# One PSUM tile handed out by the schedule, a shared buffer for the squares, stored priorities and a shorter first inverse in a Nyström attention + MLP kernel

## The chip, the cores and the metric

The kernel runs on one core of a Trainium2 chip. The metric is the device time of one execution in microseconds (us). A core has TensorE (PE; its weight loads are listed apart as PEld), VectorE (DVE), ScalarE (ACT), GpSimd (POOL) and SyncE (SP). [...]

## The reference

Queries, keys and values have 8 batches, 8 heads, 576 tokens and 64 values per head. Attention goes through 32 landmarks per head, each the mean of 18 tokens, and an inverse of a 32x32 matrix by six Newton steps. The result feeds an MLP with squared ReLU of width 2048.

```python
q_lm = q.reshape(B, H, 32, 18, D).mean(axis=3); k_lm = k.reshape(B, H, 32, 18, D).mean(axis=3)
A  = sm(q, k_lm)       # sm(a, b) = softmax(a @ b.T / 8)
Bm = sm(q_lm, k_lm)
C  = sm(q_lm, k)
Z  = Bm.T / (norm1(Bm) * norminf(Bm) + 1e-6)
for _ in range(6):
    Z = 2 * Z - Z @ Bm @ Z
x = (A @ Z @ C @ v)    # heads side by side: 4608 rows of 512
h = x @ w_in           # 512 x 2048
out = np.maximum(h, 0) ** 2 @ w_out   # 2048 x 512
```

## The kernel before

**Batches.** Eight batches go through three stages: `attention(b)`, `mlp_in(b)`, `mlp_out(b)`. The kernel never forms the attention's output. `attention` makes `AT`, the normalized left softmax in bf16 (tokens along the free dimension), and `WT`, the product of the inverse with C·v, and then multiplies `WT` with `w_in` into `G` (heads' landmarks by 2048). `mlp_in` multiplies `G` with `AT` into `h` (128 rows of the hidden width at a time, f = 0 to 15, each 576 tokens in two pieces of 288), ACT takes the ReLU into `r` (L1055) and DVE squares it into `gT` (L1058). `mlp_out` multiplies `gT` with `w_out` into tiles `o` of 128 tokens by 512 (16 matmuls each), which ACT or DVE copies out and SP stores. Names such as L1112 are lines of this kernel. Batches are paired: 576 is four tiles of 128 tokens and 64 left over, and the left-overs of an even and an odd batch make one `mid` tile, from two buffers `gTs[0]` and `gTs[1]`, as 32 matmuls on 64-column halves of the PE array (L1099, L1101).

**The planner.** Nobody writes the order of work by hand. Each operation is added to a `Plan` with its engines and costs, what it reads and writes, a priority, a PE tile mode ("full", "64x32", ...), and the PSUM rings that it takes a buffer from. `Plan.schedule` simulates a list schedule: of the ready operations it takes the one that can start first, then critical ones (the whole of `attention(0)` up to G is critical), then by priority. Priorities rise with the batch, so later batches' attention is spread between earlier batches' MLP. A change of PE's tile mode costs 98 ns in the plan (`SWITCH`). `search(700)` tries 700 random shifts of the priorities and keeps the best plan. The instructions are then issued in the plan's order on each engine, and each engine runs its own in order.

**PSUM.** Three rings of two buffers: `h` (two banks each; `mlp_in`, left scores `sa`, their sums `ss`, and G), `n` (one bank; the small matmuls of the inverse) and `o` (one bank; output tiles, and in batch 0 the key scores `sc`).

**The first attention.** Batch 0 has nothing to hide behind. k's first half comes by SP in float32 (`kst`) and is cast by both ACT and DVE; k's second half and q's two halves come through POOL's queue. While the load is under way, PE multiplies zeros (46 matmuls in `warm`). POOL makes the masks (`constants`), DVE the other constants (`constants2`, L438 to L456), which the copies of the segment sums (`part`) wait for under the key "cst". `fold_mm` (L603) adds the two halves of the sums, `b_mm` (L626) makes the landmark scores, ACT and DVE make the softmax Y0. The inverse goes through a chain of `blocks` (L657: eight 32x32 matmuls in mode "32x32") and DVE steps (`scaled`, `double`): Y1 to Y5 and Z. `cv_mm` (L872) multiplies the exponentials `EC` with v in three steps, into unused columns of the banks of the left scores (`sa`, 1), so it waits until ACT has read those (`Ea`). Four copies (`cvb`) and the reciprocal `rcv` follow, then Z4T, `u` 4 = Z4T·cvb, `u` 5 = 2·u4 + Y4·u4 (one block and one `double`, L915), `wt_mm2` (L970) = u5·Y5, a copy to `WT`, G's first 512 columns (L982), their copies (L325, L323), and the first `in_mm` at L1044. A block may be preceded by `fill` matmuls on zeros, up to its `busy` number (2 for qq 1 to 4, 1 for u 4 and 5, else 0), where the plan sees PE idle for more than 225 + 187 ns.

**Loads.** POOL issues in order: k, q, v of batch 0, w_in 0 and 1, k and q of batch 1, w_in 2 and 3, w_out 0 and 1, v of batch 1, w_out 2 and 3. Output tiles use w_out piece f // 4 for row block f, and those of batch 0 are computed in two halves of f, added by DVE.

**Later batches.** Per batch, four operations on PE are not in mode "full": the left scores `a_mm` (L824), `cv_mm` (L890), and two `g_two` (L982), each of which takes two `h` buffers and computes 2 x 512 columns of G; its second eight matmuls use a form (`again`) without a weight load of their own. The rest of the inverse runs on PE in mode "full".

Of the kernel before, what the change touches and what calls it, by code (L numbers as in the profile page):

```python
# [9 lines left out]
P = 128  # L10
# [7 lines left out]
B = 8  # L18
H = 8
# [14 lines left out]
LAG = 1.0  # L34

# [6 lines left out]
class Plan:  # L42
# [8 lines left out]
    RINGS = {"h": 2, "n": 2, "o": 2}  # L51
# [3 lines left out]
    SWITCH = 98.0  # L55
    DMA_NS_PER_BYTE = 1.0 / 410.0
    SLACK = 150.0
    FILL, HOLD = (225.0, 187.0), 1500.0
# [67 lines left out]
    def schedule(self, shift=None):  # L126
# [12 lines left out]
        ring = {r: [] for r in self.RINGS}  # L139
# [16 lines left out]
        while left:  # L156
# [11 lines left out]
            for op in ready:  # L168
                t0 = ready_at[op]
                ok = True  # L170
                if op.acq:
                    for rn in set(r for r, _ in op.acq):
                        want = sum(r == rn for r, _ in op.acq)
                        n = len(ring[rn]) + want - self.RINGS[rn]
                        for x in range(max(n - want, 0), max(n, 0)):
                            if ring[rn][x] not in freed:
                                ok = False
                                break
                            t0 = max(t0, freed[ring[rn][x]])
                    if not ok:  # L180
                        continue
                for e, dur in op.eng.items():
# [14 lines left out]
                    key = (t, not op.crit, prio[op], op.idx, dur, fill)  # L197
                    if best is None or key < best[0]:
                        best = (key, op, e, dur)
            if best is None:  # L200
                return 1e9, log
            (t, _, _, _, dur, op.fill), op, e, _ = best
# [12 lines left out]
            for rn, k in op.acq:  # L215
                ring[rn].append(k)
# [17 lines left out]
            for k in op.keys:  # L234
# [3 lines left out]
                if not pending[k]:  # L238
                    freed[k] = freed_at
        return max(op.end for op in self.ops), log  # L240

    def search(self, rounds):

        rng = random.Random(1)
        n = len(self.ops)
        best = [0.0] * n
        end, log = self.schedule(best)
        for _ in range(rounds):
            shift = list(best)
            if rng.random() < 0.5:  # L250
                a, w, d = rng.randrange(n), rng.choice((1, 3, 10, 40)), rng.gauss(0.0, 0.15)
                for i in range(a, min(a + w, n)):
                    shift[i] += d
            else:
                for _ in range(rng.choice((1, 4, 16))):
                    shift[rng.randrange(n)] += rng.gauss(0.0, 0.15)
            e, x = self.schedule(shift)
            if e <= end:
# [940 lines left out]
```

The softmax here doesn't subtract the row's maximum and nothing guards it: scores larger than these inputs give would overflow.

## Time and profile before

| | |
|---|---|
| median of 7 runs | 255.54 us (255.22 to 257.16) |
| the profiled execution | 255.47 us, span 253.8 us, mean PE clock 0.98 |
| PE busy | 243.9 us, 2701 matmuls |
| DVE, ACT, POOL busy | 174.8, 164.4, 28.3 us |
| `o` matmuls L1112 | x528, 132.0 us |
| `mid` matmuls L1099 and L1101 | x64 each |
| `in_mm` L1044 and L315 | x256 each, 67.2 us each |
| ReLU on ACT L1055, square on DVE L1058 | x128, 651 ns and 452 ns each |
| DMA | 35.59 MB; the 16 engines 90% busy or more in slices 2 to 12 of 40 |

The span runs from the first to the last instruction; the time also holds what lies around it. In the page, "PEclk" is the PE clock that was granted, in tenths, in 40 slices of 6.3 us. The stage table gives, for each stretch, the length, each engine's busy time with its number of instructions, the granted clock, the DMA share and GB/s. The timeline gives start and length in us, engine, line, operation, output<-inputs, tile shape (rows*columns of the array), operand shape, count, and in brackets the engine's idle time before it and what ended it. Matmuls overlap: the distance between starts tells PE's pace, not the length of one.

### The profile page before, as it was taken

What the parts mean: (1) busy time and instruction counts of PE and PEld (TensorE: products, weight loads), DVE (VectorE), ACT (ScalarE), POOL (GpSimd) and SP (SyncE); (2) the same over time, 40 slices, a digit from 0 to 9 for tenths busy, and PEclk for the clock granted to TensorE, in tenths of its full rate; (3) what the DMA queues carried; (4) which work ended last, traced back from release to release, by engine and by line L of the source; (5) the groups of instructions that cost most, each with busy time, mean ns of one, the idle gap of its engine ahead of it and who ended that gap; (6) DMA issues with size and microseconds to landing.
All of it is one profiled execution on the core that took longest, in us unless ns stands there. A gap on an engine that the chain in (4) does not pass through costs nothing.

```text
span 253.8 us, 6615 instructions
## 1 busy us (share of the span) xinstructions
PE 243.9 (96%) x2701; PEld 144.9 (57%) x2701; DVE 174.8 (69%) x487; ACT 164.4 (65%) x282; POOL 28.3 (11%) x51
## 2 busy tenths in 40 slices
PE   8777999999999999999999999999999999999994
PEld 7653775456644655565645565467466544565453
DVE  1865778759966898799897799979966762253000
ACT  3586798567942887677865985769688744474211
POOL 7822200003003000300300040010000000000000
PEclk9975999999999999999999999999999999999999
DMA  7999999999998998699599969996110131301233
GB/s 141 186 206 204 207 205 208 172 169 184 179 157 188 198 200 165 112 204 230 96 187 216 146 89 220 220 163 124 44 41 3 44 83 41 85 0 41 85 83 83
DMA packets 57054, 35.59 MB, mean 140 GB/s; under 512 B 29760, under 2 KB 52544, under 8 KB 57024
## 3 DMA queue, kind: packets, MB, share of 16 engines
q0 software_dynamic: 22672, 18.06, 47.5%
q1 hardware_dynamic: 34352, 17.11, 32.2%
q8 instruction: 21, 0.34, 0.5%
q14 instruction: 9, 0.07, 0.1%
HBM read 36.70 MB, written 9.44 MB: 182 GB/s over the span
## 4 chain that ended last, share of the span: by engine, by line
PE 89%; DVE 5%; ACT 2%; DMA 2%; issue 1%; DVEq 0%
PE o L1112 43%; PE h L315 14%; PE h L1044 12%; PE o L1099 6%; PE n L842 2%; PE h L982 2%; DMA kst<-in_k_dram 2%; PE n L890 1%; PE n L794 1%; PE o L315 1%; PE h L824 1%; PE n L603 1%; PE h L930 1%; DVE G L325 1%; DVE two_i L448 1%
## 5 line engine op out<-in xcount | busy, mean ns | idle before, releaser
L1112 PE MATMUL o<-w_out_bf,gT 128*128 128x512 bf16 (+1 forms) x528 | 132.0, 373 | 0.1
L1055 ACT ACTIVATE r<-h 128x576 bf16<-128x576 f32 x128 | 78.8, 651 | 21.0 <-PE h L315 18.9
L1058 DVE TENSOR_TENSOR gT<-r 128x576 bf16<-128x576 bf16 x128 | 56.6, 452 | 20.2 <-ACT r L1055 18.2
L1112 PEld LDWEIGHTS <-gT 128*128 128x128 bf16 x528 | 48.0, 98 | 39.2 <-issue 6.0
L1044 PE MATMUL h<-AT,G 128*128 128x288 bf16 x256 | 67.2, 288 | 0.6 <-DVE G L325 0.4
L315 PE MATMUL h<-AT,G 128*128 128x288 bf16 x256 | 67.2, 288 | 0.0
L323 ACT COPY o<-o 128x512 f32<-128x512 f32 (+1 forms) x27 | 15.4, 570 | 35.7 <-PE o L1112 26.4
L315 PEld LDWEIGHTS <-G 128*128 128x128 bf16 x256 | 25.2, 98 | 12.3 <-issue 0.3
L1044 PEld LDWEIGHTS <-G 128*128 128x128 bf16 x256 | 25.1, 98 | 11.4 <-DVE G L325 1.3
L323 ACT CAST G<-h 128x1024 bf16<-128x1024 f32 x17 | 17.2, 1018 | 6.4 <-PE h L982 5.4
L325 DVE CAST G<-h 128x1024 bf16<-128x1024 f32 x13 | 15.9, 1222 | 7.3 <-PE h L315 6.4
L807 DVE SCALAR_TENSOR_TENSOR st<-st,n 128x128 bf16<-128x128 bf16 x35 | 9.9, 284 | 7.6 <-PE n L794 7.6
L483 POOL COPY gate<-qT 1x1 bf16<-1x1 bf16 x6 | 1.2, 208 | 123.7 <-DMA qT<-qraw 103.5
L1099 PE MATMUL o<-w_out_bf,gT 128*64 128x512 bf16 x64 | 14.6, 380 | 0.0
L1101 PE MATMUL o<-w_out_bf,gT 128*64 128x512 bf16 x64 | 14.6, 380 | 0.0
L935 ACT ACTIVATE Ra<-h 128x576 f32<-128x576 f32 x16 | 10.3, 653 | 3.9 <-PE h L315 3.8
L462 DVE TENSOR_TENSOR Pd<-st,ones_d 128x256 bf16<-128x256 bf16 x42 | 12.1, 288 | 0.9
L946 DVE TENSOR_TENSOR AT<-Ea,Ra 128x576 bf16<-128x576 bf16 x16 | 11.7, 754 | 1.2 <-ACT Ra L939 1.0
L849 ACT ACTIVATE EC<-n 96x512 bf16<-96x512 f32 x21 | 12.0, 609 | 0.6 <-PE n L842 0.6
L923 ACT ACTIVATE Ea<-h 128x576 bf16<-128x576 f32 x16 | 9.9, 659 | 3.9 <-PE h L824 3.9
L794 PEld LDWEIGHTS <-Pd 128*128 128x128 bf16 x84 | 7.9, 97 | 6.9 <-DVE Pd L462 1.4
L1099 PEld LDWEIGHTS <-gT 128*64 128x64 bf16 x64 | 6.7, 110 | 7.1 <-issue 1.3
(174 smaller groups left out, 291.0 us busy)
## 6 DMA issues: line engine op xcount, KB each, us to landing
vraw<-in_v_dram POOLq DMA_DIRECT2D x8, 576.0 KB, 6.7
out_dram<-o SPq DMA_DIRECT2D x23, 192.0 KB, 2.5
kraw<-in_k_dram POOLq DMA_DIRECT2D x7, 576.0 KB, 9.1
qraw<-in_q_dram POOLq DMA_DIRECT2D x7, 576.0 KB, 12.7
out_dram<-o SPq DMA_DIRECT2D x24, 128.0 KB, 2.4
w_in_bf<-in_moe_w_in_dram POOLq DMA_DIRECT2D x4, 512.0 KB, 15.3
w_out_bf<-in_moe_w_out_dram POOLq DMA_DIRECT2D x4, 512.0 KB, 21.9
out_dram<-o SPq DMA_DIRECT2D x23, 64.0 KB, 2.1
```

The source lines that it names most:

```text
L315: nc.tensor.add_instruction(mybir.InstMatmult(start_tensor_calc=start, stop_tensor_calc=stop, is_transpose=transpose, ldweights=False, til ...
L323: nc.scalar.copy(dst, src)
L325: ENG[e].tensor_copy(dst, src)
L462: nc.vector.tensor_tensor(dst[:], src.unsqueeze(2).to_broadcast([P, 2, NG, M]), ones_d[:].unsqueeze(1).to_broadcast([P, 2, NG, M]), ALU.mult)
L849: nc.scalar.activation(EC[:, x, :, :, :, :].rearrange("p c i g m -> p (i g) c m"), PS[sc][0:TP, :, :].rearrange("p y (c m) -> p y c m", c= ...
L946: add(("DVE", dve_ns(S)), lambda e, i=i: nc.vector.tensor_tensor(AT[:, i, :], Ea[:, i, :, :].rearrange("p c t -> p (c t)"), Ra[:, i, :, :] ...
L1044: (again if j else nc.tensor.matmul)(t[:, j, 0:HALF], lhsT=G[:, i, f * P:(f + 1) * P], rhs=AT[:, i, j * HALF:(j + 1) * HALF], start=(i == ...
L1055: add(("ACT", act_ns(S)), lambda e, hk=hk, r=r: nc.scalar.activation(r.rearrange("p (j t) -> p j t", j=2), PS[hk][:, :, 0:HALF], AF.Relu), ...
L1058: add(("DVE", dve_ns(S, 2)), lambda e, r=r, f=f: nc.vector.tensor_tensor(gTs[z][:, f, :], r[:], r[:], ALU.mult), reads=[("r", rn)], writes ...
L1099: nc.tensor.matmul(t[0:64, :], lhsT=gTs[0][:, f, 4 * P:S], rhs=w_out_bf[:, f, :], start=(f == 0), stop=(f == NF - 1))
L1101: nc.tensor.matmul(t[64:P, :], lhsT=gTs[1][:, f, 0:64], rhs=w_out_bf[:, f, :], start=(f == 0), stop=(f == NF - 1))
L1112: nc.tensor.matmul(PS[ok][:, 0:hi - lo], lhsT=gTs[z][:, f, x0:x0 + P], rhs=w_out_bf[:, f, lo:hi], start=(f == f0), stop=(f == f1 - 1))
```

## The change

- **PSUM.** The three rings become one tile of eight banks. `Plan.room` and `Plan.take` give each buffer its banks at the planned moment: at most three `h` (a pair of neighbouring banks), three `n` and three `o` (one bank of 2 to 7, next to a busy bank first). `bank` makes the view. Batch 0's `fold_mm` takes an `o` bank, `cv_mm` has its own bank and no longer waits for `Ea`; its four copies wait for the reciprocal.
- **Squares.** One `gT` of 1152 columns for both batches of a pair: the mid tile is an ordinary tile of 16 full matmuls at columns 512 to 639.
- **Priorities.** The search is gone. A table `SHIFTS` holds one shift per operation, in steps of 1/64 between −2 and 2, and `LOADS` sets those of six loads: by their numbers, w_in 0 comes before v of batch 0, q of batch 1 before its k, and the last four loads become w_out 1, 3, 2 and v of batch 1. `STICK` makes a PE operation of another mode look 98 ns later while PE is in a tiled mode.
- **First inverse.** Y4·Y5 is formed (`yy`, `Y45` = 2·Y5 + Y4·Y5) instead of `u` 5, and WT = u4·Y45. `b_mm` gets an earlier priority. G's first 512 columns go in two halves with a copy each, and `in_mm` reads the half that it needs.
- **Fillers.** Every block, `wt_mm2`, the first g and the first `in_mm` may be preceded by up to three zero matmuls, from 160 + 187 ns of planned idle time.
- **Constants.** `constants2` is split in `fixed` (needs nothing, first on DVE), `folds`, the copy of the ones, and `doubles`.
- **Later G.** The two `g_two` become four operations of 512 columns, each with its own `h` buffer and weight loads.

The diff, cut to its core (`bank` loses its first argument everywhere; the table is left out):

```diff
+LOADS = {11: 1.0, 12: -1.0, 14: 1.0, 15: -1.0, 20: 2.0, 22: -2.0}
+SHIFTS = (
...
...
-    RINGS = {"h": 2, "n": 2, "o": 2}
+
+    KINDS = {"h": (3, 2), "n": (3, 1), "o": (3, 1)}
+    NBANKS = 8
...
-    SWITCH = 98.0
+    SWITCH, STICK = 98.0, 98.0
...
-    FILL, HOLD = (225.0, 187.0), 1500.0
+    FILL, HOLD = (160.0, 187.0), 1500.0
...
+                    if e == "PE" and mode != "full" and op.mode != mode:
+                        key = (t + self.STICK, not op.crit, prio[op], op.idx, dur, fill)
+                    else:
+                        key = (t, not op.crit, prio[op], op.idx, dur, fill)
...
+                held[rn] = [x for x in held[rn] if freed.get(x, 1e12) > t] + [k]
+                place[k] = self.take(rn, t, busy)
+                for b in place[k]:
+                    busy[b] = 1e12
...
+    def room(self, op, held, busy, freed):
+
+        t0 = 0.0
+        busy = list(busy)
+        for rn, _ in op.acq:
+            most, width = self.KINDS[rn]
+            want = sum(r == rn for r, _ in op.acq)
+            ends = sorted(freed.get(k, 1e12) for k in held[rn])
+            n = len(ends) + want - most
+            if n > 0:
+                t0 = max(t0, ends[n - 1])
+            if width == 2:
+                t, b = min((max(busy[b], busy[b + 1]), b) for b in range(0, self.NBANKS, 2))
+                busy[b] = busy[b + 1] = 1e12
             else:
-                for _ in range(rng.choice((1, 4, 16))):
-                    shift[rng.randrange(n)] += rng.gauss(0.0, 0.15)
-            e, x = self.schedule(shift)
-            if e <= end:
-                end, best, log = e, shift, x
-        return end, log
+                t, b = min((busy[b], b) for b in range(2, self.NBANKS))
+                busy[b] = 1e12
+            t0 = max(t0, t)
+        return t0
+
+    def take(self, rn, t, busy):
+
+        if self.KINDS[rn][1] == 2:
+            b = next(b for b in range(0, self.NBANKS, 2) if max(busy[b], busy[b + 1]) <= t)
+            return (b, b + 1)
+        return (min((busy[b ^ 1] <= t, busy[b], b) for b in range(2, self.NBANKS) if busy[b] <= t)[2],)
+
+    @staticmethod
+    def shifts(n):
+
+        if not SHIFTS:
+            return [0.0] * n
+        table = base64.b85decode(SHIFTS)
+        assert len(table) == n
+        moves = [(x - 128) / 64.0 for x in table]
+        for op, x in LOADS.items():
+            moves[op] = x
+        return moves
...
+    psall = psum.tile([P, Plan.NBANKS, 512], F32, name="ps")
+    pairs = [psall[:, 2 * i:2 * i + 2, :] for i in range(Plan.NBANKS // 2)]
...
+    u4 = sb.tile([P, 2, D], BF16, name="u4")
+    Y45 = sb.tile([P, 2, M], BF16, name="Y45")
...
-    gTs = [sb.tile([P, NF, S], BF16, name="gT%d" % i) for i in range(2)]
+    gT = sb.tile([P, NF, 2 * S], BF16, name="gT")
...
+    def fixed(e):
+        nc.vector.memzero(qpad[:])
         nc.vector.memzero(bdq[:])
         nc.vector.memzero(cvb[:])
-        nc.vector.memzero(qpad[:])
         nc.vector.memset(ones_1[:], 1.0)
         nc.vector.memset(eps[:], 1e-6 / M)
         nc.vector.memset(v1[:, :, D:D + 2], 1.0)
-        for g in range(NG):
-            r = slice(M * g, M * g + M)
-            for i in range(2):
-                nc.vector.tensor_scalar(out=two_i[r, i, :], in0=ident[r, r], scalar1=2.0, scalar2=None, op0=ALU.mult)
         for nm in ("k", "q"):
             for T in Ts[nm]:
                 nc.vector.memzero(T[:, TW:TW + P - TP])
+
+    def folds(e):
         for i in range(2):
             for j in range(2):
                 nc.vector.tensor_copy(fold[64 * i:64 * i + 64, 64 * j:64 * j + 64],
                                       ident[64 * i:64 * i + 64, 64 * i:64 * i + 64])
-        nc.vector.tensor_copy(ones_d[:], ones_f[:])
+
+    def doubles(e):
+        with nc.allow_low_precision("ones and zeros"):
+            nc.vector.reduce_sum(two_1[:], ident.rearrange("p (g m) -> p m g", g=NG), axis=AX.X)
+        for i in range(2):
+            nc.vector.tensor_scalar(out=two_i[:, i, :], in0=two_1[:], scalar1=2.0, scalar2=None, op0=ALU.mult)
...
+    def idle(t, k=0, m=0):
+
+        if plan.now.fill:
+            warm(t, plan.now.fill)
+            if k:
+                nc.tensor.matmul(t[0:m, 0:D], lhsT=zeros[0:k, 0:m], rhs=zeros[0:k, 0:D], start=True, stop=True,
+                                 skip_group_check=True)
...
+                acq=(("o" if first else "n", fp),), prio=at(pk + 0.05))
...
+            acq=(("n", bm),), prio=at(0.1 if first else 0.2), mode="128x32" if first else "full", words=16)
...
-        def blocks(key, lhs, rhs, reads, pi, busy=0, dim=M):
+        def blocks(key, lhs, rhs, reads, pi, busy=3, dim=M):
 
             def go(e):
-                t = bank("n", key, [P, 512])
-                if plan.now.fill:
-                    warm(t[:, 2 * D:512], plan.now.fill)
-                    nc.tensor.matmul(t[0:M, 2 * D:3 * D], lhsT=zeros[0:M, 0:M], rhs=zeros[0:M, 0:D], start=True,
-                                     stop=True, skip_group_check=True)
+                t = bank(key, [P, 512])
+                idle(t[:, 2 * D:512], M, M)
...
-                t = PS[(A, "sa", 1)][:, :, 512 - 2 * D - 1:512]
-                PS[cv] = t
+                if j == 0:
+                    bank(cv, [P, 2, 2 * D + 1])
+                t = PS[cv]
...
+                add(("PE", 8 * 41.0), lambda e, j=j: cv_mm(e, j), reads=[("EC", j), "cst"] + vkeys,
+                    writes=[cv], acq=((cring, cv),) * (j == 0), prio=at(0.42), mode="128x64", words=24)
...
+            reads=[cv], writes=["rcv", "sums"], prio=at(0.43))
...
-            blocks((A, "u", 5), Ys[4], us[0], yk(4) + [("u", 4)], at(0.44), busy=1, dim=D)
-            double(us[1], us[0], (A, "u", 5), [("u", 4)], [("u", 5)], at(0.44), n=128)
+            blocks((A, "yy"), Ys[4], Ys[5], yk(4) + yk(5), at(0.42))
+            double(Y45, Ys[5], (A, "yy"), yk(5), ["Y45"], at(0.42))
...
+                            nc.tensor.matmul(t[64 * i:64 * i + 64, x, 0:M], lhsT=u4[r, i, :], rhs=Y45[r, i, :],
...
+                parts_n = 2 if n == 0 else 1
+                w = 512 // parts_n
+                for y in range(parts_n):
+                    gp = [(A, "g", n, y, i) for i in range(1 if tag == "h" else 2)]
+                    kind = "o" if y else tag
+
+                    def g_one(e, n=n, gp=gp, tag=tag, y=y, w=w):
+                        ts = g_bank(gp[0]) if tag == "h" else [bank(x, [P, 512]) for x in gp]
+                        if n == y == 0:
+                            idle(ts[0], 64, M)
+                        g_mm(e, n, ts, cols=(w * y, w * y + w))
+
+                    add(("PE", pe_ns(w) + 25.0), g_one, reads=["WT0", "WT1", ("wi", n)],
+                        writes=gp, acq=tuple((kind, x) for x in gp), prio=at(0.6 + 0.1 * n), mode="64x32",
+                        words=16, pre=3 * (n == y == 0))
...
+                gp = (A, "g", n)
+                add(("PE", pe_ns(512) + 25.0), lambda e, gp=gp, n=n: g_mm(e, n, g_bank(gp)),
+                    reads=["WT0", "WT1", ("wi", n)], writes=[gp], acq=(("h", gp),), prio=at(0.62 + 0.2 * (n // 2)),
+                    mode="64x32", words=16)
...
+            tiles = [(4 * P, [(0, b - 1, 4 * P, 64), (64, b, 0, 64)])]
+            tiles += [(5 * P + t * P, [(0, b, 64 + t * P, P)]) for t in range(4)]
...
-                    if x0 is None:
-                        def mid(e, ok=ok):
-                            t = bank("o", ok, [P, DM])
-                            for f in range(NF):
-                                nc.tensor.matmul(t[0:64, :], lhsT=gTs[0][:, f, 4 * P:S], rhs=w_out_bf[:, f, :],
-                                                 start=(f == 0), stop=(f == NF - 1))
-                                nc.tensor.matmul(t[64:P, :], lhsT=gTs[1][:, f, 0:64], rhs=w_out_bf[:, f, :],
-                                                 start=(f == 0), stop=(f == NF - 1))
-
-                        add(("PE", NF * (pe_ns(DM) + 6.0)), mid,
-                            reads=[("gT", i, f) for i in range(2) for f in range(NF)] + [("wo", j) for j in range(4)],
-                            writes=[ok], acq=(("o", ok),), prio=pr, mode="128x64", words=64)
...
+                            nc.tensor.matmul(PS[ok][:, 0:hi - lo], lhsT=gT[:, f, x0:x0 + P],
+                                             rhs=w_out_bf[:, f, lo:hi], start=(f == f0), stop=(f == f1 - 1))
...
+    add(("DVE", 2500.0), fixed, writes=["bdq0", "bdq1", "cst"], prio=-300.0)
+    add(("DVE", 500.0), folds, reads=["ident"], writes=["fold"], prio=-5.0)
+    add(("DVE", 220.0), lambda e: nc.vector.tensor_copy(ones_d[:], ones_f[:]), reads=["onesf"], writes=["ones"], prio=-4.99)
+    add(("DVE", 540.0), doubles, reads=["ident"], writes=["two_i"], prio=-4.6)
```

## Prediction

> **What bounds the kernel now.** I read the page first, then a table of stages, the timeline of TensorE at the stages' borders, the waits of the first 24 us, and the landings of the loads. The page:
>
> ```profile
> span 253.8 us, 6615 instructions
> ...
> PEclk9975999999999999999999999999999999999999
> ...
> PE 89%; DVE 5%; ACT 2%; DMA 2%; issue 1%; DVEq 0%
> ```
>
> TensorE (PE) holds the end, and its clock is not full in slices 3 and 4. The stages, cut where the clock changes and where the first `in_mm` starts (23.79):
>
> ```profile
> core 0: us, PE busy (x) PEld busy (x) DVE busy (x) ACT busy (x) POOL busy (x), PEclk, DMA share, GB/s
> 0.00:16.10 16.10, 12.65 (x255) 10.86 (x255) 9.20 (x43) 8.78 (x15) 10.92 (x24) 1.00 1.05 173
> 16.10:23.79 7.69, 5.15 (x125) 2.84 (x120) 4.82 (x19) 4.60 (x12) 2.28 (x3) 0.50 1.30 205
> 23.79:26.34 2.55, 2.55 (x21) 1.84 (x22) 0.73 (x2) 1.43 (x2) 0.79 (x1) 0.50 1.24 207
> ...
> 45.00:250.00 205.00, 204.92 (x2022) 116.53 (x2020) 144.85 (x376) 132.40 (x223) 13.50 (x22) 1.00 0.73 130
> 250.00:253.80 3.80, 0.13 (x2) 0.00 (x0) 0.00 (x0) 0.37 (x1) 0.00 (x0) 1.00 0.29 80
> ```
>
> Until 23.79 a chain through small matmuls and DVE steps sets the time; from there PE streams without a pause; the tail is one copy and one store. Half clock rules from 16.10 to 26.34. So there are three places to gain: an earlier 23.79, the half clock, and what PE loses between matmuls later. The end of the first chain on PE:
>
> ```profile
> 20.02 0.29 PE L657 MATMUL n<-cvb,Z4T 32*32 32x64 bf16 x8
> 20.96 0.29 PE L657 MATMUL n<-u,Y 32*32 32x64 bf16 x8 [0.65 <-DVE u L325]
> 21.64 0.26 PE L970 MATMUL h<-Y,u 32*64 32x32 bf16 x8 [0.39 <-DVE u L664]
> 22.35 0.63 PE L982 MATMUL n<-w_in_bf,WT 64*32 64x512 bf16 x8 [0.45 <-ACT WT L323]
> ...
> 23.79 0.42 PE L1044 MATMUL h<-AT,G 128*128 128x288 bf16 x1 [0.39 <-DVE G L325]
> ```
>
> Each step waits for one evacuation. A later place, at full clock, shows what PE loses in the long stage:
>
> ```profile
> 48.30 0.81 PE L1112 MATMUL o<-w_out_bf,gT 128*128 128x512 bf16 x3
> 49.05 0.41 PE L982 MATMUL h<-w_in_bf,WT 64*32 64x512 bf16 x8
> 49.27 0.40 PE L315 MATMUL h<-w_in_bf,WT 64*32 64x512 bf16 x8
> 49.60 1.68 PE L1112 MATMUL o<-w_out_bf,gT 128*128 128x512 bf16 x7
> ```
>
> A plain `o` matmul starts every 0.216 (7 of an undisturbed run took 1.51). The three at 48.30 took 0.75 instead of 0.65, the two groups of g 0.55 instead of 0.43. So one trip into another tile mode and back costs 0.10 + 0.12 = 0.22. Batches 1 to 7 make four trips each (a, cv, two g) and there are four `mid` tiles: 32 trips, 7.0 us. Comparing all starts after 26.34 with the undisturbed pace of their kind, PE loses 12.4 us, of which the tail is 3.8; the trips are nearly all of the rest.
>
> [...] the trace has ACT waiting 0.7 for DVE's copy of `cvb` from the same bank. [...] No overlap of memsets with GpSimd's issue of loads is in this trace (DVE is idle from 1.2 to 5.4)[...].
>
> **The change part by part.**
>
> *Constants split.* Before, `constants2` runs on DVE from 6.01 to 10.26 and k's means leave only at 9.93 (`fold_mm` of k at 10.40). `fixed` needs nothing and goes into DVE's idle time; `folds`, the ones and the doubled identity (8 small ones of 1.50 become 3) lie between 6.0 and 8. k's fold could go near 9.2. But q's second half lands at 10.38, so q becomes the limit: before, 12 transposes (0.51) go first, then means (0.46), copy (0.27), fold, `b_mm` at 12.03. With free banks (k's fold takes an `o` bank) and `b_mm` ahead of q's fold, means can start at 10.45: `b_mm` near 11.4. Worth 0.6, never more than 0.8; if the transposes stay first, 0.2.
>
> *Loads.* Swaps: w_in 0 before v0, q1 before k1, w_out 3 before w_out 2, v1 last. v0 landed at 14.01 and w_in 0 at 16.28; v0 will land near 16.3. w_in 0 is not needed before 19. Batch 0's `cv_mm` needs v0: a new wait on PE, and `cvb`, the reciprocal, Z4T and u4 are queued behind it. It replaces a wait of the same length: before, steps 2 and 3 of `cv_mm` started at 16.38, after Ea was read from the shared banks.
>
> *cv in its own bank.* `cv_mm` is three steps of 0.42 at full clock (the first, 15.11) or 0.64 at half (two from 16.38 to 17.7). From 16.35: end 17.8 with latency, or 18.5. Then reciprocal 0.17 and four copies of 0.26 to 0.28 in turn from one bank, as before (17.96 to 19.29): u4 near 19.2, or 19.9, against 20.02. The Y chain itself, 0.6 earlier and without `cv_mm` in its way, would be ready near 17, so it no longer sets u4.
>
> *Inverse shortened.* The block and doubling at 20.96 go: 0.68. Y4 times Y5 and `Y45` (one block, one DVE step of 0.21) run beside u4 and its copy; Y5 is long done. Were it late, at most 0.7 would come back. The copy of u4 waited behind the 0.75 of AT on DVE: up to 0.3 more.
>
> *First g in halves.* G's first 256 columns: the copy falls from 0.69 to 0.43, its matmul by 0.1: 0.3 off the path, for one more copy on each engine beside PE work.
>
> From u4 to `in_mm` it was 3.77. Less 0.68, 0.3, 0.3 and some 0.3 for full clock, 2.2: `in_mm` at 21.4, say **21.5**, 2.3 earlier. With half clock, 22.2.
>
> *Fillers.* All blocks, WT, g and the first `in_mm` may take up to three 384-column dummies of 0.16. Some 5 us of gaps hold about ten of them; before there was one. [...] I take it that the clock stays full until PE streams. That frees the 2.55 at half clock, 1.25. Bounds: −1.25 to +2 (the fillers double at half clock).
>
> *Supply.* The loads keep their pace: w_in 2 and 3 landed at 28.21 and 30.80, w_out from 33.32. PE has about 14 us of work without w_out (16 `in_mm` of 0.49, k1 and q1 3.4, the rest of batch 1's attention 3), so from 21.5 to 35.5: just enough; but ACT was busy 9.6 of 10 in 30 to 40. I add 0.5; between 0 and 2.3.
>
> *Squares in one buffer.* The mid tile took 3.57 as 32 half-width matmuls, 16 full ones take 3.45; [...]0.21 × 4 = 0.85 less. No new wait: the tile needed both batches before.
>
> *Banks, priorities.* The g pairs become single operations with weights loaded again. Side by side they cost no more trips; apart, 14 × 0.22 = 3.1 more. The rule that keeps PE in its mode, and shifts of up to two batches, can join trips: at best one per batch, 1.5. I take 0.8 less; range −1.5 to +3.1. Three h pairs instead of two are hidden: PE has no wait for h in the long stage. The tail is not touched.
>
> *Sum.* 253.8 − 2.3 − 1.25 + 0.5 − 0.85 − 0.8 = 249.1. The profiled execution took 255.47, 1.67 more than its span, and the median is 255.54, as good as equal: **250.8**.
>
> **The rivals.**
> A, *the clock still falls* until about 26.3: `in_mm` at 22.2 (−1.6), and the streaming before 26.34 loses 4.1/2 = 2.07, not 1.25 (+0.8): 253.8 − 1.6 + 0.8 + 0.5 − 0.85 − 0.8 = 251.85, time 253.5. For it: the gaps hold one dummy each[...].
> B, *the start brings nothing*: v0 comes late or PE runs dry before w_out, the landings set the pace, and only the mid tiles and joined trips less split g are left, about 0.85: 254.6. For it: the loads' queue is full until 50; against it: PE had work from 23.79 on.
> C, *slower: h gets one pair.* Single-bank tiles may sit in banks 2 to 7; spread over three pairs they leave banks 0 and 1 to h. A round trip is then 0.49 + 0.27 + ACT 0.65 + 0.1 = 1.5. Stage 45 to 250 gives 1.83 per h (112). If ACT answers 0.4 later, as behind a G copy of 1.02, a trip takes 1.9: 112 × 0.07 = 8, less the forecast's 4.7: 258.8. It decides from 1.87 up. Against it: singles are placed beside busy singles first.
> D, *more trips joined* and fuller early stage: 248.5.
>
> **How the numbers follow.** Forecast 0.49, A 0.27, B 0.10, C 0.08, D 0.06. 0.5% (1.3 us) is about what a measurement can tell from no change: faster means below 254.3, slower above 256.8. Faster: forecast, D, 0.26 of A and 0.02 of B: 0.83; same 0.09; slower 0.08. Range 248.4 to 254.6: it leaves out C, half of D and some of B.
>
> **What would show it.** First `in_mm` at 21 to 22; no stretch of half clock between 12 and 27, with zero-matmuls in the chain; no block between u4's copy and WT; `cv_mm` starting with v0's landing near 16.3; mid tiles as 16 full matmuls; trips of 0.22, at most 28. Wrong would be: half clock while PE streams, gaps before 36, g in four separate trips, or PE waiting for relu in the long stage.

## The result and the profile after

The changed kernel takes 253.47 us (median of 23 runs, 252.60 to 255.05) against 256.13 us for the kernel before in the same comparison (median of 60, 254.51 to 258.13). The ratio is 0.9896 with an interval of 0.9878 to 0.9914: faster by 1.04%, where the prediction said 1.9%. Runs that lie more than 1.5% above the fastest of their kernel are left out of all medians and ratios. The profiled execution took 252.70 us, 1.70 more than its span.

The page of the kernel after, to be held against the three lines of the page before (253.8 us, the clock "9975...", PE 89% of the chain):

```profile
span 251.0 us, 6542 instructions
...
PEclk9999999999999999999999999999999999999999
...
PE 82%; DMA 13%; POOL 2%; issue 1%; ACT 0%; DVE 0%; POOLq 0%
```

The granted clock is full in every slice. The share of PE in the chain that ended last fell and DMA's rose from 2% to 13%: the early part of the chain now runs through loads. The stages, cut at the first `in_mm` (22.37, before 23.79), at the point where before's half clock ended, and at the last matmuls:

```profile
core 0: us, PE busy (x) PEld busy (x) DVE busy (x) ACT busy (x) POOL busy (x), PEclk, DMA share, GB/s
...
16.10:22.37 6.27, 5.01 (x141) 2.73 (x141) 4.19 (x17) 4.51 (x13) 1.60 (x3) 1.00 1.29 205
22.37:26.34 3.97, 3.97 (x54) 3.37 (x55) 2.47 (x7) 3.97 (x8) 0.75 (x2) 1.00 1.27 207
26.34:45.00 18.66, 17.88 (x239) 11.39 (x239) 15.57 (x44) 14.53 (x26) 1.46 (x2) 1.00 1.26 206
45.00:247.05 202.05, 201.93 (x1996) 115.89 (x1986) 141.95 (x374) 133.51 (x228) 13.57 (x22) 1.00 0.73 132
247.05:251.00 3.95, 0.17 (x2) 0.00 (x0) 0.00 (x0) 0.37 (x1) 0.00 (x0) 0.89 0.25 71
```

PE streams at full clock from 22.37. In 26.34 to 45.00 it is idle for 0.78 us, where before it was idle for 0.18. The chain that ended last, in order of time (start, length, what), names what it waits for:

```profile
7.31 11.75 DMA w_in_bf<-in_moe_w_in_dram
19.35 21.59 DMA w_out_bf<-in_moe_w_out_dram
40.98 1.46 PE ps L1179 x6
```

Until 40.98 this chain is one queue of loads behind another; neither the inverse nor the first `in_mm` is on it. The timeline of PE shows the first of the two places where the queue is felt (`w_in` piece 2 landed at 27.78):

```profile
27.83 0.41 PE L1061 MATMUL ps<-w_in_bf,WT 64*32 64x512 bf16 x8 [0.70 <-DMA w_in_bf<-in_moe_w_in_dram]
```

The second is at 40.98, where the next matmul was due at 40.74 by PE's pace and `w_out` piece 2 landed at 40.94; counted from the end that the trace gives the matmul before it, the idle time is 0.08, and 0.70 + 0.08 is the 0.78 of the stage. From 40.98 on the chain is PE alone. The end of the first chain, in the timeline of all engines, weight loads left out:

```profile
19.19 0.23 DVE L983 TENSOR_TENSOR Z4T<-ps,rcv 128x64 bf16<-128x64 f32 x1
...
19.33 0.21 DVE L801 TENSOR_TENSOR Y<-ps,y4p 128x64 bf16<-128x64 f32 x1
...
19.46 0.32 PE L560 MATMUL ps<-zeros 128*128 128x384 bf16 x1 [0.87 <-DVE Z4T L983]
19.63 0.32 PE L380 MATMUL ps<-zeros 128*128 128x384 bf16 x1
...
19.89 0.25 PE L732 MATMUL ps<-cvb,Z4T 32*32 32x64 bf16 x8
...
20.20 0.29 DVE L390 CAST u<-ps 128x128 bf16<-128x128 f32 x1 [0.66 <-PE ps L732]
20.26 0.39 PE L560 MATMUL ps<-zeros 128*128 128x512 bf16 x1
20.41 0.21 DVE L739 SCALAR_TENSOR_TENSOR Y<-Y,ps 128x64 bf16<-128x64 bf16 x1
20.49 0.38 PE L380 MATMUL ps<-zeros 128*128 128x512 bf16 x1
...
20.80 0.22 PE L1048 MATMUL ps<-Y,u 32*64 32x32 bf16 x8
...
22.37 0.30 PE L1123 MATMUL ps<-AT,G 128*128 128x288 bf16 x1 [0.24 <-DVE G L390]
```

The block between u4's copy and WT is gone, as meant. But the zero matmuls (L560, L380) are themselves on the chain. PE stood idle for 0.87 us ahead of u4's block, and the fillers did not use that gap: the first starts at 19.46, when Z4T was ready (19.42), and u4's block only at 19.89. The trace names Z4T as what ended the idle time before the first filler. The kernel's plan, worked out from its code, gives the block and its fillers the bank that Z4T reads; that this shared bank is what held them back was not shown, since no run gave them another. WT's matmuls need u4's copy (ready at 20.49) and Y45 (the line at 20.41, ready at 20.62), and start at 20.80, behind two more fillers. The fillers ahead of g end about when WT's copies do (21.45) and cost next to nothing. A trip into another tile mode, in the chain (length from one start to the next):

```profile
50.40 0.65 PE ps L1179 x3
51.04 0.77 PE ps L1061 x24
51.81 0.97 PE ps L1179 x4
```

Twenty-four matmuls of g (undisturbed 0.64) took 0.77, and the four of `o` after them 0.97 instead of 0.86: 0.23 for the trip, the same price as before. Here three operations of g share one trip. Over the whole kernel, after the first `in_mm`, there are 28 stays in another mode where there were 34. Five of the 34 and one of the 28 followed another tiled group directly, so the changes of mode fell from 63 to 55.

### The profile page after: what moved, and what is told of

Same layout as the page of the kernel before. It is cut to its first block, busy times and chain, and to the rows that moved or that the text cites. A ratio compares the mean times of both kernels' runs of the same rounds, so it can differ in the third digit from the quotient of the medians.

```text
span 251.0 us, 6542 instructions
## 1 busy us (share of the span) xinstructions
PE 241.5 (96%) x2658; PEld 143.5 (57%) x2658; DVE 173.1 (69%) x479; ACT 164.0 (65%) x287; POOL 28.5 (11%) x51
## 4 chain that ended last, share of the span: by engine, by line
PE 82%; DMA 13%; POOL 2%; issue 1%; ACT 0%; DVE 0%; POOLq 0%
PE ps L1179 49%; PE ps L380 12%; PE ps L1123 11%; DMA w_out_bf<-in_moe_w_out_dram 9%; DMA w_in_bf<-in_moe_w_in_dram 5%; PE ps L1061 3%; PE ps L917 2%; PE ps L966 1%; PE ps L869 1%; PE ps L899 1%; PE ps L1006 1%; POOL qraw L456 1%; PE ps L681 1%; PE ps L707 0%; POOL ones_f L494 0%
## 5 line engine op out<-in xcount | busy, mean ns | idle before, releaser
L1179 PE MATMUL ps<-w_out_bf,gT 128*128 128x512 bf16 (+1 forms) x592 | 144.9, 374 | 0.1
L1135 ACT ACTIVATE r<-ps 128x576 bf16<-128x576 f32 x128 | 76.2, 660 | 11.6 <-PE ps L380 9.9
L1123 PE MATMUL ps<-AT,G 128*128 128x288 bf16 x256 | 65.8, 286 | 0.2 <-DVE G L390 0.2
L380 PE MATMUL ps<-AT,G 128*128 128x288 bf16 x256 | 65.7, 286 | 0.0
L388 ACT COPY o<-ps 128x512 f32<-128x512 f32 (+1 forms) x30 | 17.0, 571 | 42.3 <-PE ps L1179 38.2
L380 PEld LDWEIGHTS <-G 128*128 128x128 bf16 x256 | 25.0, 98 | 10.4 <-issue 0.2
L388 ACT CAST G<-ps 128x1024 bf16<-128x1024 f32 (+2 forms) x22 | 19.4, 940 | 5.8 <-PE ps L1061 5.7
L390 DVE CAST G<-ps 128x1024 bf16<-128x1024 f32 (+2 forms) x14 | 14.9, 1070 | 8.5 <-PE ps L1061 8.4
L882 DVE SCALAR_TENSOR_TENSOR st<-st,ps 128x128 bf16<-128x128 bf16 x35 | 10.0, 285 | 10.8 <-PE ps L869 10.7
L924 ACT ACTIVATE EC<-ps 96x512 bf16<-96x512 f32 x24 | 13.2, 604 | 0.5 <-PE ps L917 0.5
L1011 ACT ACTIVATE Ra<-ps 128x576 f32<-128x576 f32 x16 | 10.3, 653 | 3.5 <-PE ps L380 3.3
L1061 PE MATMUL ps<-w_in_bf,WT 64*32 64x512 bf16 (+1 forms) x264 | 10.2, 374 | 0.7 <-DMA w_in_bf<-in_moe_w_in_dram 0.7
L560 PE MATMUL ps<-zeros 128*128 128x128 bf16 (+2 forms) x52 | 6.3, 286 | 2.6 <-DVE zeros L482 1.3
```

Source lines behind the costliest of these rows:

```text
L380: nc.tensor.add_instruction(mybir.InstMatmult(start_tensor_calc=start, stop_tensor_calc=stop, is_transpose=transpose, ldweights=False, til ...
L388: nc.scalar.copy(dst, src)
L390: ENG[e].tensor_copy(dst, src)
L924: nc.scalar.activation(EC[:, x, :, :, :, :].rearrange("p c i g m -> p (i g) c m"), PS[sc][0:TP, :, :].rearrange("p y (c m) -> p y c m", c= ...
L1061: nc.tensor.matmul(ts[i][M * g:M * g + M, lo:hi], lhsT=WT[64 * i:64 * i + 64, g, :], rhs=w_in_bf[64 * i:64 * i + 64, g, n * 512 + lo:n * 5 ...
L1123: (again if j else nc.tensor.matmul)(t[:, j, 0:HALF], lhsT=G[:, i, f * P:(f + 1) * P], rhs=AT[:, i, j * HALF:(j + 1) * HALF], start=(i == ...
```

## The experiments

All of them are edits of the kernel after, unless "before" is named. Where two kernels are compared at equal clock, the mean granted clock of each timed run was used: it lies mostly near 1.000, 0.993, 0.986, 0.980, 0.973 or 0.966, in steps of 0.0067 or about 1.7 us of the span. That is what 3.41 us at half clock take away, and single stretches of half clock in the traces are that long (21.56 to 24.97 with the long inverse, 22.74 to 26.15 with fillers in the kernel before).

**Does the start still set the end?** Six zero matmuls delay the first `in_mm`; nothing else changes.

```diff
+                if b == f == 0:
+                    warm(t[:, 0, :], 6)
```

> The changed kernel with six more zero matmuls of 512 columns before the first in_mm, which then starts about 1.0 us later (near 23.4 instead of 22.37). Theory 'chain': the end moves by the same 1.0 us, since PE has no pause afterwards. Theory 'supply': PE waits for w_in 2 near 27.8 and for w_out 2 near 40.9 anyway, 0.9 us in all, so the end moves by 0.1 to 0.4 us.

The first `in_mm` came at 23.16, 0.79 later, and the wait for `w_in` 2 disappeared. Time 253.28 (252.60 to 254.78), ratio 0.9891 (0.9854 to 0.9928), span 250.9 at full clock: nothing lost. The delay was paid out of the wait. Two of the six timed runs, at a mean clock of 0.993, had spans of 253.0 and 253.1, where the kernel after has 251.4 at that clock: with the wait spent, lost clock seems to reach the end in full.

**Is the shortened inverse worth its 0.68?** In the same plan u5 is formed again between u4 and WT, and the block Y4·Y5 is not issued.

```diff
+                        nc.tensor.matmul(t5[r, i, :], lhsT=Ys[4][r, i, :], rhs=u4[r, i, :], start=True, stop=True)
+                nc.vector.scalar_tensor_tensor(out=u5[:], in0=u4[:], scalar=2.0, in1=t5, op0=ALU.mult, op1=ALU.add)
...
-                            nc.tensor.matmul(t[64 * i:64 * i + 64, x, 0:M], lhsT=u4[r, i, :], rhs=Y45[r, i, :],
+                            nc.tensor.matmul(t[64 * i:64 * i + 64, x, 0:M], lhsT=u5[r, i, :], rhs=Ys[5][r, i, :],
```

> The kernel after in the same plan, with the first inverse as long as before: u5 = 2*u4 + Y4*u4 is formed by one block and one DVE step between u4 and WT, and the block Y4*Y5 and its step are not issued. Supply theory (the loads set the pace after 22.4): the first in_mm starts some 0.7 us later, near 23.1, the wait of 0.70 for w_in 2 at 27.8 shrinks by as much, and the span stays within 0.2 us of 251.0. Chain theory (my prediction took the 0.68 as saved one for one): span 251.6 to 251.8, time 0.7 us above the kernel after.

253.41 us (252.52 to 256.02), ratio 0.9895 (0.9832 to 0.9959). The profiled run had a stretch of half clock (mean 0.989, first `in_mm` 23.88, span 252.2), but the two timed runs at full clock had spans of 250.8 and 250.9, where the kernel after has 251.2 (median of 13). With the loads as they are, the shorter inverse buys nothing that these runs resolve.

**Is it the order of two loads?** `w_in` 2 (operation 16) is issued ahead of k of batch 1 (operation 14). The list has the loads' operation numbers in the order in which GpSimd issues them; without the edit 14 stands before 16.

```diff
+        want = [12, 11, 13, 15, 16, 14, 17, 18, 19, 22, 21, 20]
...
+        for x, op in zip(at, want):
+            log[x] = rows[op]
```

> The kernel after in the same plan, with one load moved: w_in 2 is issued before k of batch 1, all else as it was. Single-wait theory (the 0.70 us at 27.8 is a wrong order of two loads): w_in 2 lands near 25.2, the wait goes and nothing comes in its place: 0.7 us less, ratio 0.987. Supply theory (PE has then all the work that the loads allow): the wait moves on, to k of batch 1 or to w_out 2 at 40.9, which grows from 0.24 to about 0.9: within 0.2 us of the kernel after.

253.54 us (252.61 to 255.44), ratio 0.9897 (0.9865 to 0.9929), profiled span 251.0 at full clock. `w_in` 2 landed at 24.41 and its wait went. These two came in its place (timeline of PE, that kernel's own line numbers; the first is for `w_in` 3, the second for `w_out` 2, landed at 40.92):

```profile
29.93 0.41 PE L1066 MATMUL ps<-w_in_bf,WT 64*32 64x512 bf16 x8 [0.53 <-DMA w_in_bf<-in_moe_w_in_dram]
...
40.97 1.46 PE L1184 MATMUL ps<-w_out_bf,gT 128*128 128x512 bf16 x6 [0.52 <-DMA w_out_bf<-in_moe_w_out_dram]
```

The two waits now sum to 1.05, and the first `in_mm` came at 22.08. Put side by side, the start of the first `in_mm` plus PE's idle time for loads after it is 22.37 + 0.78 = 23.15 in the kernel after, 22.08 + 1.05 = 23.13 here, and 23.16 with the delay. The spans are 251.0, 251.0 and 250.9. A start earlier than about 23.2 is handed back as a wait. The same sum works throughout: in eight profiles of this plan, the span less the first `in_mm`, less the waits for loads and less half of the half-clock time after it, is 227.6 to 227.9 us.

**Lighter loads.** Half of the columns of `w_in` 2 and 3 and of `w_out` 2 and 3 are left out of the loads and set to zero in SBUF, so this kernel leaves part of the MLP's weights out of the computation; once with the zeros written by GpSimd, once by DVE, and once with the delay of the first experiment as well.

```diff
...
-                w_out_bf[:, 4 * j:4 * j + 4, :],
-                moe_w_out[512 * j:512 * j + 512, :].rearrange("(ft fp) c -> fp ft c", fp=P))
+                w_out_bf[:, 4 * j:4 * j + 4, 0:w],
+                moe_w_out[512 * j:512 * j + 512, 0:w].rearrange("(ft fp) c -> fp ft c", fp=P))
```

> The changed kernel, but w_in 2 and 3 and w_out 2 and 3 load only half of their columns and the rest is zero: the computation leaves these weights out. Each of the four lands earlier, the last by some 5 us. Theory 'supply': the waits for w_in 2 (0.7 us) and w_out 2 (0.2) go, the end comes 0.7 to 1.0 us earlier. Theory 'chain': the loads don't matter, less than 0.2 us.

> The half loads once more (the computation leaves out half of the columns of w_in 2 and 3 and w_out 2 and 3, as zeros), but with the zeros written by DVE in its idle time before the first load lands instead of by GpSimd between its loads, so that the start is that of the changed kernel (first in_mm near 22.4). Theory 'supply': PE's waits for w_in 2 and w_out 2 (0.9 us) go, the span is 250.0 to 250.4 at full clock instead of 251.0 to 251.4. Theory 'chain': no difference beyond 0.2 us.

> Both: the half loads of four weights (left out weights as there) and the 1.0 us of zero matmuls before the first in_mm. Theory 'supply': with the loads early, the delay is no longer absorbed: 0.8 to 1.0 us later than with the half loads alone. If the delay is again absorbed, something else than the loads takes it up.

254.08 (251.74 to 254.77), 253.08 (251.98 to 255.21) and, with the delay, 253.02 us (252.37 to 255.88). The medians say nothing, because about half of these runs lost clock or started late (first `in_mm` at 26.12 and 26.18 in two of the profiles). The runs at full clock fit the supply: spans of 250.0, 250.0 and 250.6 with light loads (three runs only), 251.1 with light loads and the delay (median of ten), and with full loads 251.2 without and 251.3 with it. So the delay seems to cost most of its 0.8 once the loads are light, and 0.1 while they are not. Three runs are too few to call this shown. The profile of the second version points the same way: no wait for a load after its first `in_mm` at 23.64, and a span of 251.4.

**What do the fillers buy?** The same plan, with the planned zero matmuls left out.

```diff
         for op, e, _, op.end in log:
+            op.fill = 0
             self.now = op
```

> The changed kernel with the same plan, but none of the planned zero matmuls in the first chain (the 46 before the first load stay, and the three before q). Theory 'clock': the dummies hold the clock; without them half clock returns for about 10 us from some 16 us on, as before the change, and the time rises by 1 to 2 us. Theory 'dummies in the way': they stand before u 4, WT and the first g and start late, so without them the first in_mm comes 0.4 to 0.6 us earlier than 22.37; at full clock the time falls by up to 0.5 us.

253.90 us (253.01 to 254.66), ratio 0.9902 (0.9869 to 0.9934). The clock fell in all runs (mean 0.971 to 0.986; half clock from 18.61 to 25.44 in the profile). Yet the first `in_mm` came at 22.46, only 0.09 later than with fillers at full clock, although v of batch 0 landed 0.72 later in this profile (17.12 against 16.40). The place ahead of u4 (this kernel's own line numbers):

```profile
19.67 0.23 DVE L984 TENSOR_TENSOR Z4T<-ps,rcv 128x64 bf16<-128x64 f32 x1
...
19.95 0.29 PE L733 MATMUL ps<-cvb,Z4T 32*32 32x64 bf16 x8 [0.65 <-DVE Z4T L984]
```

From Z4T to u4's block it takes 0.06 here, and 0.47 or 0.48 in the four profiles of this plan that have the fillers and full clock there; so those two fillers cost 0.42. From the start of `cv_mm` to the first `in_mm` it is 5.30 without fillers, most of it at half clock, and 5.70 with fillers at full clock. On this stretch the fillers cost more than half clock does. What half clock costs comes after it: the `in_mm` matmuls start every 0.24 us up to 25.44 and every 0.12 us behind it, so 1.5 us of streaming, of which the waits for loads, now gone, absorb some 0.8. Beside the delayed kernel of the same comparison (253.28, ratio 0.9891) the fillers are worth 0.3 us by the ratios and 0.6 by the medians, less than the intervals can tell from nothing.

**Fillers in the kernel before.** At least one in front of each block of the first inverse.

```diff
-                if plan.now.fill:
-                    warm(t[:, 2 * D:512], plan.now.fill)
+                if first:
+                    warm(t[:, 2 * D:512], max(1, plan.now.fill))
```

> The kernel before the change, with its own plan, but at least one zero matmul of 384 columns ahead of each block of the first inverse (before: one block had one). Theory 'clock': the kernel before loses most of its time against the changed one by half clock alone, which these dummies prevent: granted clock 0.99 or more instead of 0.97 to 0.98, and the time falls by 1.2 to 2.5 us, so that 0 to 1 us is left to the changed kernel. Theory 'chain and bookkeeping' (shorter inverse, mid tiles, stored priorities): the dummies only lengthen the chain by 0.2 each where PE had no gap; the time stays within 0.6 us.

256.58 us (254.66 to 258.36, 16 runs), ratio 1.0011 (0.9981 to 1.0041). The clock rose to a mean of 0.987 at the median, from 0.973, and to 1.000 in two runs, but the first `in_mm` moved to 24.24 in the profile, and at a clock near 0.986 the span is 255.1 (seven runs) where the kernel before has 253.2. Here the clock alone brought nothing, because the chain paid for it.

**The mid tile, alone in the kernel before.** One buffer of 1152 columns and 16 full matmuls per mid tile, in before's own plan.

```diff
-                                nc.tensor.matmul(t[0:64, :], lhsT=gTs[0][:, f, 4 * P:S], rhs=w_out_bf[:, f, :],
...
-                                nc.tensor.matmul(t[64:P, :], lhsT=gTs[1][:, f, 0:64], rhs=w_out_bf[:, f, :],
+                                nc.tensor.matmul(t[:, :], lhsT=gT[:, f, 4 * P:5 * P], rhs=w_out_bf[:, f, :],
```

> The kernel before in its own plan; only the squares of both batches are in one buffer and each of the four mid tiles is 16 full matmuls instead of 32 on halves of the array. My prediction's step: 4 x 0.21 = 0.85 us less, ratio 0.9967 (half of the time after 2% of clock noise: 0.995 to 0.998). Rival (the halves run side by side at no loss[...]): within 0.2 us of before, ratio 0.999 to 1.001.

254.70 us (253.87 to 256.70), before 256.62, ratio 0.9939 (0.9911 to 0.9968): more than expected. Spans at equal clock say why (medians, number of runs in brackets; the last two columns belong to the experiment after next):

| mean clock | before | before, full mid tile | after, searched | after |
|---|---|---|---|---|
| 0.997 and up | none | none | 251.2 (1) | 251.2 (13) |
| near 0.993 | none | none | none | 251.4 (5) |
| near 0.986 | 253.2 (23) | 252.6 (7) | 252.5 (9) | 252.2 (4) |
| near 0.980 | 254.1 (13) | 253.2 (6) | 253.1 (6) | 252.4 (2) |
| near 0.973 | 254.9 (45) | 254.2 (4) | 254.2 (4) | none |
| near 0.966 | 256.1 (29) | 255.0 (1) | none | none |

The mid tile alone brings 0.6, 0.9, 0.7 and 1.1, weighted by its runs 0.75. The rest, 0.8 by the ratio and 1.2 by the medians, is a higher clock in these 18 runs; why a change so far from the start should bring that stays open.

**The mid tile in halves again, in the kernel after.** Each of the sixteen steps of a mid tile is two half-width matmuls.

```diff
-                            nc.tensor.matmul(PS[ok][:, 0:hi - lo], lhsT=gT[:, f, x0:x0 + P],
...
+                            for c in ((0, 64), (64, P)) if x0 == 4 * P else ((0, P),):
+                                nc.tensor.matmul(PS[ok][c[0]:c[1], 0:hi - lo], lhsT=gT[:, f, x0 + c[0]:x0 + c[1]],
...
```

> The changed kernel, same plan, but each of the four mid tiles again as 32 matmuls on halves of the array. The prediction's step: 0.21 us each, the time rises by 0.85 us. They run after 60 us, where PE has no pause, so nothing can absorb it: the end moves by 0.7 to 0.9 us.

258.80 us (258.19 to 261.14), ratio 1.0119 (1.0066 to 1.0172). This missed what it was meant to measure. After the change the steps of a mid tile are operations of their own, and the plan puts others between them, so that the halves fell into 26 groups, each with a trip into another mode and back. At full clock the span was 256.5, 5.3 more than after: 0.20 per group, about the price of a trip. Before, the 32 halves of a mid tile were issued as one block, and so paid such a price once per tile.

**The stored priorities.** First all of them set to zero (the order of the loads kept), then 700 random trials as before, started from there.

```diff
-        moves = [(x - 128) / 64.0 for x in table]
+        moves = [0.0 for x in table]
...
-        end, log = self.schedule(self.shifts(len(self.ops)))
+        end, log = self.search(700)
```

> The changed kernel with all stored shifts of the priorities at zero and the order of the six loads kept; the plan is then made anew. It has one trip into another tile mode more (33 against 32, the first chain's included). If the stored priorities are worth what the prediction put on joined trips, the time rises by 0.2 to 0.8 us; if they are worth most of the change, by 2 us or more, with new waits of PE.

> The kernel after with the stored priorities replaced by what before did: 700 random trials, here started from no shifts (the order of the loads kept). Theory that the stored priorities are worth more than such a search can find: 255.5 to 257 us, ratio 0.997 to 1.003, between the run with no shifts and before. Rival (no shifts at all was an unlucky plan, and any search brings the gain): 253.5 us, ratio 0.99, the clock at 0.99 or above.

With zeros 257.33 us (255.93 to 257.86), ratio 1.0036 (1.0015 to 1.0058): slower than before. With the search 254.70 us (253.63 to 256.88), ratio 0.9938 (0.9911 to 0.9966), neither theory's number. The page and the first `in_mm` with the search:

```profile
PEclk9955999999999999999999999999999999999999
```

```profile
24.66 0.30 PE L1143 MATMUL ps<-AT,G 128*128 128x288 bf16 x1 [0.21 <-DVE G L410]
```

So most of the 3.9 us between zeros and the table is what this one search found: 2.6 us. The table is worth 1.2 us more than its 700 trials (1.1 by the ratios). In the profiles the searched plan starts streaming 2.3 us later, after half clock in slices 3 and 4. From there to the end it needs 252.9 − 24.66 = 228.2 us; the kernel after needs 228.6, of which 0.78 are waits for loads. At equal clock it is where the kernel before with the full mid tile is (252.5 and 252.6, 253.1 and 253.2, 254.2 and 254.2 in the table above). Under a plan found as before's was, the parts other than the mid tile bring nothing that shows in the spans; with the table they and the order of the work bring the rest together. Most of that rest is clock: 18 of 24 runs with the table had a mean of 0.993 or more, and 1 of 20 with the search, while at equal clock the two are 0 to 0.7 us apart. The profiles offer a reason that was not tested alone: the plans with zeros and with the search have no filler between 9 and 19 us, where the table's plan has four (12.48 to 16.25), and their half clock begins at 14.0 and 13.8.

## Why the prediction was right in sign and too large

The forecast of 250.8 had the direction and the places right, and the range of 248.4 to 254.6 holds the time. Two steps failed in the main. The first `in_mm` came 1.42 us earlier instead of 2.3, and about half of the missing 0.9 is fillers that were taken as free and stood on the chain; and the waits for loads were added as a constant of 0.5, where the runs show a floor that hands back what an early start gains. Together these two bring −0.64 instead of −1.8, which is 1.2 of the 1.9 us by which the sum misses the span; most of the rest lies in the joined trips. The sum, against what the two profiles and the runs show:

| term | forecast | measured |
|---|---|---|
| first `in_mm` earlier | −2.3 | 23.79 − 22.37: −1.42 |
| half clock gone after it | −1.25 | half of 2.55: −1.27 |
| waits for loads | +0.5 | PE idle: +0.78 |
| mid tiles | −0.85 | −0.6 (profile) to −0.75 (runs), full mid tile in before |
| trips joined, and the rest | −0.8 | what is left of −2.8: −0.1 to −0.3 |
| span | 249.1 | 251.0 |

**First `in_mm`.** The landmarks (`b_mm` 11.92, said 11.4) and v0 (landed 16.40, said 16.3; `cv_mm` done at 17.8, as said) were nearly right. u4 came at 19.89 instead of 19.2: Z4T, the last of the evacuations in turn, was ready at 19.42, and the two fillers in front of u4 added 0.42. From u4 to `in_mm` it took 2.48 instead of 2.2; the fillers ahead of WT hold at most 0.13 of it. "Y5 is long done" did not hold either: `cv_mm` and the queue of DVE stood before it, Y5 came at 19.54, after Z4T, and WT waited for Y45 0.13 longer than for the copy of u4. The step that failed took the fillers for free because they lie in gaps. Their cost was entered only for the case that the clock falls (they "double at half clock"; in the traces the starts of two 512-column fillers lie 0.23 us apart at full clock, from 20.26 to 20.49, and 0.40 at half clock, from 21.90 to 22.30 with the long inverse), never for the case that a filler starts after the gap. One thing more sets this start: v0, moved behind w_in 0. In six profiles of this plan `cv_mm` begins 0.04 us after v0 landed, and that landing varied from 16.37 to 17.64, so that −1.42 is one draw. The memsets that `fixed` moved ahead (1.28 to 2.53) held nothing up: GpSimd issues k and q at 1.37 and 2.16, in 0.80 and 1.33 us, in both traces.

**Supply.** The step was there, and its bounds of 0 to 2.3 hold the value; its size was 0.5 against 0.78. The worse error is in how it was joined to the others. It was added as a constant to a gain of 2.3, but it is a floor: what the start gains beyond about 23.2 comes back as waiting. So only some 0.6 of the start's gain could reach the end, and the runs with a later `in_mm` and with the long inverse end with the same span at full clock. Had the start come at 21.5 as forecast, this floor would have made the waits some 1.7, by an estimate from 23.2 − 21.5. The sign "gaps before 36" that the prediction set for being wrong is there, at 27.83. Rival B, "the landings set the pace", was given one chance in ten; it is the right mechanism, joined with the gain of clock that it left out.

**Clock.** It held, as forecast; rival A fell. With the fillers the early slices of the page are full; without them slice 4 shows 5 tenths, and all six timed runs have a mean of 0.971 to 0.986, where 18 of 24 with fillers have 0.993 or more. The lost clock comes in portions of 3.41 us: 10.24 in the kernel before (16.10 to 26.34, granted clock 0.50) and 6.83 without the fillers (18.61 to 25.44). That some ten fillers would be enough was the author's estimate; how many it takes, and where they must stand, no run measured. But the 1.25 was not net: with the fillers left out the whole kernel is only 0.3 to 0.6 us slower.

**Mid tiles.** Right: 0.85 was forecast, four times 0.21. Of that, 0.12 is the difference of the two lengths, and the other 0.09 fits the time by which a mid tile starts late in the trace before (at 235.98, where the ten `o` matmuls from 233.73 at a pace of 0.216 lead to 235.89). In the kernel before it is 0.75 by the runs at equal clock. By the sum used above for the span, its two profiles give 228.7 and, with the full mid tile, 228.1.

**Trips.** The price was right (0.23 against 0.22), and the bound of "at most 28" after the first `in_mm` was met at its edge. But 0.8 was the value of four joined trips, and beyond the four of the mid tiles only two were joined, at most 0.44. With 0.15 lost at the tail (3.95 after 3.80), that is about −0.3, as the sum leaves. No run measured this term alone. The price is measured between starts; what PE does in that time the traces do not show.

**Rival C** (h left with one pair of banks) and rival D (more joined) did not come: stage 45 on shows PE busy for 201.93 of 202.05 us.

**From span to median.** The terms miss the span by 1.9. The median of the runs lies another 0.77 above the profiled execution, much as for the kernel before (256.13 against 255.47); so the ratio of the two profiled executions, 0.9892, is that of the medians. The spread is the clock: none of 110 runs of the kernel before had a mean above 0.987, while 18 of 24 of the kernel after had 0.993 or more. Starting from one profile at 0.98 took a middling execution for the typical one, which is at 0.973.

What stays open: which of the table's shifts hold the clock was not taken apart, and the split of G's first columns, the bank allocation, the split constants, `STICK` and the new order of the loads were not undone alone. No version that these runs point to beats the kernel after: with the full mid tile and a held clock it stands on the floor of its loads.

## What to carry to other kernels

Before adding up gains at the start of a kernel, put the landings of the loads beside the work that they allow: here a start earlier than about 23.2 was handed back as a wait, and the gain was capped, not reduced by a constant. A filler that is to keep the clock up should not be counted as free before the trace shows it inside the gap. Look whether it starts before or after the thing that the next step waits for: here the two ahead of u4 stood behind an empty gap of 0.87 us and added 0.42, and from `cv_mm` to the first `in_mm` the chain took 5.70 us with fillers at full clock and 5.30 without them, most of it at half clock. When a change brings its own order of work, run it once under the order's old quality as well, or the order's merit is booked on the parts.

## What the runs showed that was not expected

Lost clock came in equal portions: the mean clocks of most runs lie near steps of 0.0067, or 3.41 us at half clock, and in the kernel before each portion costs about 1.0 us of span (253.2, 254.1, 254.9, 256.1). The kernel before never ran without at least two of them. A half-width tile whose steps are spread between other work costs 0.20 us per group; as one block it costs 0.2 per tile (0.75 over the four of the kernel before). And the same program varied in its portions from run to run, between none and two or three in the kernel after, so medians of few runs compare draws of the clock before they compare kernels.
